# First group of an FNet and quick-GELU kernel: steps 2 to 7 built in one PSUM bank by a seed and two matrices, and the middle column's weights taken from summed rows

## Chip, cores and metric

One NeuronCore of a Trainium2 chip. The metric is the device time of one execution in microseconds (us). All arithmetic is in float32.

## What is computed

```python
X = np.fft.fft(x, axis=1)             # x: (8, 3008, 256), float32
X = np.fft.fft(X, axis=2)
x = X.real.astype(np.float32).reshape(8 * 3008, 256)
h = x @ w_in                          # w_in:  (256, 2048)
g = h * (1.0 / (1.0 + np.exp(-1.702 * h)))
out = (g @ w_out).astype(np.float32)  # w_out: (2048, 256)
```

The real part of a two-dimensional Fourier transform, then two matrix products with a sigmoid form of GELU between them. The kernel takes `w_in` and `w_out` as 64-bit numbers and makes float32 of them itself.

## The kernel before

The transform over the 3008 rows is done in two stages (47 x 64). The first folds rows and multiplies by a table on TensorE; its output is written to a DRAM scratch `Td` (`spill_first`) and read back in another order (`fill`, line 358, tile `t`, 512 KB a piece). `rotate` (psr) treats the middle column of it, and `stage2` (line 378, ps) makes the second stage; VectorE transposes the result into `pq` (line 385), which has two parts, the cosine part `pq[:, 0]` and the sine part `pq[:, 1]`. The transform over the 256 columns is folded into the weights: `fold_w(n)` multiplies a quarter of `w_in` (512 hidden units) by a cosine and sine table `cd` into psw and copies it to `wcs[0]` and `wcs[1]` on ScalarE (line 508). For quarters 1 to 3 it works on sums and differences of two row halves (`halved`, lines 480 and 481, on VectorE).

A step t is two blocks of 128 hidden units on 256 columns of output rows. Eight steps (NP = 8) are a group; 48 groups make the batch of 8 (three blocks `blk` and two halves `hh` each). Each hidden unit is needed for a row and for its mirrored row: with pa = `wcs[0]`ᵀ`pq[:, 0]` and pb = `wcs[1]`ᵀ`pq[:, 1]`, plus a term of one middle column (`nb`, a copy of row 0 of the sine part broadcast to all partitions, times a weight per hidden unit, `af1` and `af2 = 2 af1`), they are a sum and a difference. `first_row(n)` computes those weights per hidden unit for quarter n with 16 matmuls of one column (psf) and copies them on ScalarE (lines 516, 517).

The kernel has two ways to do it:

- In the first group (steps 0 to 7): `hidden(t)` puts pa and pb into two PSUM banks and copies pa to `v` on ScalarE (line 552); `rows(t)` adds v and pb on VectorE (582), forms `dif` from `nb`, `af2` and pb (587, twice) and adds it to pa (589); `activate(t)` applies GELU to both halves at once (593, 128x1024, in place). Row 0 of `wcs[1]` is not cleared until `no_row`, which has two DMAs.
- From step 8 on: `middle(t)` seeds one bank x with `nb` times `af1` on ScalarE (602, two instructions); `begin(t, 0)` and `begin(t, 1)` add both matrices into the same bank; between the two, `doubled(t)` copies twice the bank to `g` (614, ScalarE); `forward(t)` applies GELU to the bank (617), `backward(t)` subtracts it from g on VectorE (621), `activate_back(t)` applies GELU to that (624). Here row 0 of `wcs[1]` has to be zero.

`product(t, lo, hi)` multiplies the activated rows by `w_out` (o, line 191; all matmuls but those of line 378, 501, 701 go through the helper `halves`, line 191, each as two halves of 64 columns). From step 8 the products use a form with fewer matmuls, which needs differences of `w_out` (`differences`, line 493 on GpSimd; `small_weights`, line 712 on VectorE) and of the activations (632, 633, 639, 640).

Conversion of a chunk of weights (four of `w_in`, in0 to in3; four of `w_out`, out0 to out3) takes these operations of 128x1024: `sizes` (absolute value of the upper word, on ScalarE, line 429, or on VectorE, line 431), `clamp` (GpSimd, 435), `low` (lower word scaled, ScalarE, 439), `high` (two on VectorE, 454 and 455), and `finish`: `finish_in` (467) or `finish_out` (475, two), both on GpSimd. `bounds` is prepare, sizes on ScalarE, clamp, low.

Nothing is scheduled automatically: each engine executes its instructions in the order in which the program issues them, and that order is written by hand. Ahead of step 0 it is a straight list; for steps 0 to 7 it is `SCRIPT`, one list per step, after which the operations in `extra` for that step are issued (loads, `differences(i)` after steps 5 to 8, `small_weights(i)` after steps 7 to 10, `stage2` of the next block after step 8); from step 8 it is the loop's own order. A product is issued three steps (LAG = 3) after its hidden values. PSUM banks are handed out in turn from the list `spare`; `ring` does the same for SBUF buffers, of which the ring "h" (activated rows) shares its memory with `made`, the first stage's output that `spill_first` writes to DRAM. `warm(n)` issues n matmuls of 128x512 on one weight tile whose result nobody reads.

Of the kernel before, what the change touches and what calls it, by code (L numbers as in the profile page):

```python
# [27 lines left out]
F32 = mybir.dt.float32  # L28
# [91 lines left out]
def kernel(ctx: ExitStack, tc, x, w_in, w_out, tab1, tab2, out):  # L120
# [33 lines left out]
    af1, af2 = (const.tile([128, NF], F32, tag=f"af{i}", name=f"af{i}") for i in (1, 2))  # L154
    ones = const.tile([128, 128], F32, tag="ones", name="ones")
    twos = const.tile([128, 1], F32, tag="twos", name="twos")

    psu = ExitStack()
    o_banks = [psp.tile([128, 512], F32, tag=f"o{i}", name=f"o{i}") for i in range(2)]
# [16 lines left out]
    def bank(name, tag=None):  # L176
        if tag is None:
            tag = spare.pop(0)
            spare.append(tag)
        if tag in ("o0", "o1"):  # L180
            return o_banks[int(tag[1])]
        return (rest if tag[0] == "o" else psp).tile([128, 512], F32, tag=tag, name=name)
# [5 lines left out]
    def halves(out, lhs, rhs, **how):  # L188

        for c0 in (0, 64):  # L190
            nc.tensor.matmul(out[c0:c0 + 64], lhsT=lhs[:, c0:c0 + 64], rhs=rhs, skip_group_check=True, **how)  # L191
# [142 lines left out]
    def spill_first(k, m0, m1, engines):  # L334
        for c, eng in enumerate(engines):
            eng.dma_start(out=view(Td[0], (NJ * m0 + 16 * c + 12 - 4 * k) * D, [NJ * D, m1 - m0], [1, 4 * D]),
                          in_=made[k][64 * c + m0:64 * c + m1].rearrange("p q d -> p (q d)"))
# [3 lines left out]
            for p0, p1 in ROWS:  # L341
                nc.sync.dma_start(out=w1[64 * r + p0:64 * r + p1, :], in_=tab1[p0:p1, n0 + 4:])

    def warm(n):

        ps = bank("warm")
        for _ in range(n):
            nc.tensor.matmul(ps[:], lhsT=wcs[0][:, 0:128], rhs=wcs[0][:, 0:512], start=True, stop=True)

# [10 lines left out]
    def rotate(b, a0=0, a1=NG, copy=None):  # L360

        col = t4t[b][:, a0:a1, H]
        ps = bank("psr")
        halves(ps[:, 0:a1 - a0], rot, col, start=True, stop=True)
        (copy or nc.vector.tensor_copy)(col, ps[:, 0:a1 - a0])
# [111 lines left out]
    def halved(n):  # L477

        s = summed[n] = pre["in", n][0]
        nc.vector.tensor_tensor(s[:, 0:512], wst[n][:, 0], wst[n][:, 1], op=ALU.add)  # L480
        nc.vector.tensor_tensor(s[:, 512:], wst[n][:, 0], wst[n][:, 1], op=ALU.subtract)
# [29 lines left out]
    def first_row(n):  # L511

        ps = bank("psf")
        for f in range(4 * n, 4 * n + 4):
            halves(ps[:, f:f + 1], wcs[1][:, f * 128:f * 128 + 128], twos[:], start=True, stop=True)
        nc.scalar.copy(af2[:, 4 * n:4 * n + 4], ps[:, 4 * n:4 * n + 4])
        nc.scalar.activation(af1[:, 4 * n:4 * n + 4], ps[:, 4 * n:4 * n + 4], ACTF.Copy, scale=0.5)


    def no_row(c0):  # L520
        nc.sync.dma_start(out=wcs[1][0:1, c0:c0 + 1024], in_=tab1[127:128, n0 + 4:n0 + 1028])

    NP = NF // 2
    steps = [(b, blk, hh, p) for b in range(B) for blk in range(NBLK) for hh in range(2) for p in range(NP)]
# [19 lines left out]
    def hidden(t):  # L544

        n = width(t)
        pa, pb = (bank(name, f"b{i}" if t == NP - 3 else None) for i, name in enumerate(("pa", "pb")))
        for ps, cs in ((pa, 0), (pb, 1)):
            for i in range(2):
                halves(ps[:, i * 256:i * 256 + n], *operands(t, cs, i), start=(i == 0), stop=(i == 1))  # L550
        v = sp.tile([128, 512], F32, tag="v", name="v")
        nc.scalar.copy(two(v[:], n), two(pa[:], n))
        vb[t] = v, pa, pb
# [37 lines left out]
    def activate(t):  # L591
        g = free(ht[t][:], 0, [256, 4], [1, width(t)])
        nc.scalar.activation(g, g, ACTF.Gelu_apprx_sigmoid)

    def middle(t):

# [297 lines left out]
    for i, need in enumerate(((0, 7), (1,), (6,), (2,), (5,), (3,), (4,), ())):  # L894
        for g in need:
            fold_first(g)
        mix_first(i)
        if i == 0:
            warm(3)
            spare[:] = spare[5:] + spare[:5]  # L900
        if i % 2:
            spill_first(i // 2, 0, 16, (nc.sync, nc.scalar))
        if i == 3:
            sizes(in0, nc.scalar, 0, 512)
            clamp(in0, 0, 512)
        if i in (4, 7):
            low(in0, 512 * (i // 7), 512)
        if i == 6:
            sizes(in0, nc.vector, 512, 512)
            clamp(in0, 512, 512)  # L910
            for h0 in (0, 512):
                high(in0, h0, 512)
# [16 lines left out]
    load_out(1, nc.sync)  # L929
    fill(0, 4, NG)  # L930
    warm(1)
    fold_w(0)
    halved(1)
    rotate(0, 0, 4, nc.scalar.copy)
    prepare(out0)
    sizes(out0, nc.scalar)
# [19 lines left out]
    out1, in3, out2, out3 = ("out", 1), ("in", 3), ("out", 2), ("out", 3)  # L956
    for t, c in ((1, 2), (3, 3)):
        at(t, load_out, c, nc.sync)
    at(3, no_row, 0)
    at(3, load_matrices)  # L960
    if B > 1:
        for k in range(3):
# [9 lines left out]
    for b in range(B):  # L972
# [26 lines left out]
        for blk in range(NBLK):  # L999
            nxt = (b, blk + 1) if blk + 1 < NBLK else (b + 1, 0)  # L1000
            if nxt[0] < B:
                at(t0 + blk * NF + 8, stage2, *nxt)
                at(t0 + blk * NF + 9, nyquist_out, *nxt)
                at(t0 + blk * NF + 10, nyquist, *nxt)

    SCRIPT = (
        [(prepare, in2), (low, in2), (nyquist, 0, 0), (rows, 0, ((sizes, in2, nc.vector), (clamp, in2)))],
        [(first_row, 1), (activate, 0), (rows, 1), (high, in2), (finish, in2)],
        [(activate, 1), (rows, 2), (halved, 2)],
        [(product, 0, 0, None), (product, 1, 0, None), (bounds, out1), (activate, 2), (bounds, in3), (rows, 3), (activate, 3),  # L1010
         (fold_w, 2), (high, out1), (finish, out1), (high, in3), (finish, in3)],
        [(first_row, 2), (rotate, 0, 4, NG, nc.scalar.copy), (rows, 4), (halved, 3)],
        [(product, 2, 0, None), (activate, 4), (bounds, out2), (rows, 5), (activate, 5), (fold_w, 3), (high, out2), (finish, out2)],
        [(first_row, 3), (product, 3, 0, None), (bounds, out3), (rows, 6), (activate, 6), (high, out3), (finish, out3)],
        [(product, 4, 0, None), (rows, 7)])
    for t in range(n + LAG):
        if t < NP:
            if t == NP - 3:
                spare[:] = [tag for tag in spare if tag[0] == "o"] + ["b2"]
            if t == NP - 1:  # L1020
                middle(NP)
            hidden(t)
            if t == NP - 1:
                begin(NP)
                no_row(1024)
            for fn, *args in SCRIPT[t]:
                fn(*args)
            if t == NP - 1:
                doubled(NP)
                middle(NP + 1)  # L1030
        else:
            after, special = (any(fn in (mix1, stage2) for fn, _ in extra.get(k, ())) for k in (t - 1, t))
            if t < n:
                begin(t, 1)
            if t == NP:
                activate(t - 1)
            if after and t + 1 < n:
                middle(t + 1)
            if t < n:
                forward(t)  # L1040
            while waiting:
                m, ps = waiting.pop()
                mixed(m, 1, ps)
            opening = (t - LAG) % NP == 0 and t >= NP + LAG
            one, other = (t - LAG, (1, 2, 4, 7)), (t - LAG - 1, (5, 6, 3))
            if opening:
                small_products(*other)
            cut = 0 if opening and not after else 3 if after else 2
            product(t - LAG, 0, cut)
            if after:  # L1050
                small_products(one[0], one[1][:1])
                small_products(other[0], () if opening else other[1][:1])
            if t + 1 < n:
                begin(t + 1)
            if not opening:
                small_products(other[0], other[1][after:])
            product(t - LAG, cut, 6 if t - LAG == last else None)
            small_products(one[0], one[1][after:])
            swap(t - LAG - 2)
            if t < n:  # L1060
                backward(t)
            if t + 1 < n:
                doubled(t + 1)
            if t < n:
                activate_back(t)
                sums(t, nc.gpsimd)
            if t + 2 < n and not special:
                middle(t + 2)
            combine_small(t - LAG - 1)
            if t - LAG == last:  # L1070
                product(last, 6, None)
            sums(t - 1, nc.vector)
            deeper(t - 2, 0)
            deeper(t - 3, 1)
        if t == NP:
            psu.close()
            low = ctx.enter_context(tc.tile_pool(name="low", bufs=1, space=PS))
            pot["low"] = low.tile([128, 3 * 512], F32, tag="low", name="low")
        if t >= LAG:
            combine(t - LAG)  # L1080
            combine_last(t - LAG - 2)
            turn_last(t - LAG - 3, 0)
            turn_last(t - LAG - 4, 1)
        if t >= NP:
            spare[:] = [f"b{t % 2}"] * special + ["b2"]
        for fn, args in extra.get(t, ()):
            fn(*args)
# [28 lines left out]
```

## Time and profile before

| | us |
|---|---|
| median of 3 timed runs | 1846.71 |
| lowest and highest of them | 1846.24, 1849.34 |
| profiled execution, its time | 1845.24 |
| profiled execution, span from first to last instruction | 1843.5 |
| TensorE busy | 1826.2 |
| VectorE busy | 1479.1 |
| ScalarE busy | 1139.4 |
| GpSimd busy | 997.7 |

The mean granted TensorE clock of the profiled execution is 0.997 of full speed. PE is the TensorE matmul, PEld its weight load, DVE is VectorE, ACT ScalarE, POOL GpSimd, SP the sync engine that issues most DMAs. A row of a timeline gives the start, the length, engine and line, the operation, output and input tiles, shape and how many; a bracket gives the idle time of that engine just ahead and the instruction or DMA that ended it. Line numbers are those of the kernel before.

### The profile page before, as it was taken

The page shows a single profiled execution, that of the slowest core. Times are in us where ns is not written, and L with a number is a line of the kernel's source. Part 1 is how long each engine was busy: PE and PEld are TensorE (multiplying, and loading weights), DVE is VectorE, ACT ScalarE, POOL GpSimd, SP SyncE. Part 2 cuts the span into 40 slices and gives each one's busy share as a digit, 9 for nine tenths or more (in the row PEclk, how much of TensorE's full clock was granted, in tenths as well). Part 3 has the DMA queues.
Part 4 walks back from the last instruction along what each step waited for, and adds up shares of the span by engine and source line. Part 5 has one row for each costly group of instructions (what it writes and reads, how often), then busy time and mean ns, then how long its engine had stood idle before and what let it go on. Part 6 is the DMA issues. An engine that isn't in the chain of part 4 may idle for free.

```text
span 1843.5 us, 55849 instructions
## 1 busy us (share of the span) xinstructions
PE 1826.2 (99%) x23650; PEld 1398.9 (76%) x23650; DVE 1479.1 (80%) x1930; ACT 1139.4 (62%) x2231; POOL 997.7 (54%) x1068
## 2 busy tenths in 40 slices
PE   8999999999999999999999999999999999999998
PEld 4677777777777777777777777777777877778776
DVE  6888788887888778877888778878888788878874
ACT  4666656666666666666666666666656666556663
POOL 3785555554656546564456644666446654444442
PEclk9999999999999999999999999999999999999999
DMA  8721331114211151211502115020241102100101
GB/s 276 189 70 26 90 65 28 55 32 106 43 48 40 35 112 30 61 35 45 111 13 73 33 50 97 23 72 26 75 74 28 29 26 59 28 19 13 23 19 24
DMA packets 150841, 105.95 MB, mean 57 GB/s; under 512 B 106197, under 2 KB 131799, under 8 KB 150032
## 3 DMA queue, kind: packets, MB, share of 16 engines
q1 hardware_dynamic: 147760, 100.33, 22.6%
q8 instruction: 186, 3.05, 0.7%
q10 hardware_dynamic: 2832, 2.05, 0.5%
q14 instruction: 63, 0.52, 0.1%
HBM read 65.07 MB, written 48.05 MB: 61 GB/s over the span
## 4 chain that ended last, share of the span: by engine, by line
PE 95%; POOL 2%; DMA 1%; DVE 1%; issue 0%; ACT 0%; ACTq 0%; DVEq 0%; POOLq 0%; SPq 0%
PE x L191 35%; PE o L191 26%; PE low L701 25%; PE o L701 4%; PE ps L268 2%; PE ps L378 1%; DMA xt<-in_x_dram 1%; PE po L191 0%; DMA big<-in_moe_w_in_dram 0%; PE psw L501 0%; POOL wo L475 0%; PE pa L191 0%; POOL wo L493 0%; POOL big L632 0%; DMA t<-Td 0%
## 5 line engine op out<-in xcount | busy, mean ns | idle before, releaser
L632 POOL TENSOR_TENSOR big<-big 128x256 f32<-128x256 f32 (+1 forms) x376 | 353.6, 940 | 785.7 <-ACT big L624 672.2
L191 PE MATMUL x<-pq,wcs 128*64 128x256 f32 (+1 forms) x6016 | 768.8, 376 | 1.5 <-ACT g L614 0.9
L191 PE MATMUL o<-big,wo 128*64 128x256 f32 (+1 forms) x4800 | 621.0, 375 | 0.5 <-DVE big L639 0.5
L191 PEld LDWEIGHTS x<-pq,wcs 128*64 128x64 f32 x6016 | 414.1, 137 | 181.4 <-issue 15.6
L614 ACT ACTIVATE g<-x 128x512 f32<-128x512 f32 (+1 forms) x376 | 221.7, 590 | 380.1 <-PE x L191 378.9
L191 PEld LDWEIGHTS o<-big,wo 128*64 128x64 f32 x4800 | 341.8, 137 | 146.8 <-DVE big L639 0.9
L633 POOL TENSOR_TENSOR big<-big 128x256 f32<-128x256 f32 (+1 forms) x376 | 411.2, 1094 | 0.0
L621 DVE TENSOR_TENSOR big<-g,x 128x512 f32<-128x512 f32 (+1 forms) x376 | 250.7, 667 | 183.6 <-ACT big L617 183.4
L602 ACT ACTIVATE x<-nb,af 128x256 f32<-128x256 f32 (+1 forms) x752 | 353.0, 469 | 70.1 <-DVE pq L385 57.0
L701 PE MATMUL low<-big 128*64 128x128 f32 (+1 forms) x5888 | 381.4, 270 | 0.0
L701 PEld LDWEIGHTS low<-big 128*64 128x64 f32 x5888 | 336.9, 137 | 28.2
L617 ACT ACTIVATE big<-x 128x512 f32<-128x512 f32 (+1 forms) x376 | 219.2, 583 | 122.2 <-PE x L191 112.2
L663 DVE TENSOR_TENSOR big<-big 128x1024 f32<-128x1024 f32 (+1 forms) x184 | 235.4, 1280 | 65.9 <-PE low L701 43.1
L624 ACT ACTIVATE big<-big 128x512 f32<-128x512 f32 (+1 forms) x376 | 231.6, 616 | 34.9 <-DVE big L621 32.6
L701 PE MATMUL low<-big,wo 128*64 128x128 f32 (+1 forms) x2944 | 220.3, 270 | 0.1
L665 DVE TENSOR_TENSOR big<-big 128x512 f32<-128x512 f32 (+1 forms) x184 | 179.6, 976 | 16.3 <-DVE big L663 0.5
L667 DVE TENSOR_TENSOR big<-big 128x512 f32<-128x512 f32 (+1 forms) x184 | 184.0, 1000 | 0.0
L701 PEld LDWEIGHTS low<-big,wo 128*64 128x64 f32 x2944 | 171.8, 137 | 4.2 <-DVE big L667 0.5
L640 DVE TENSOR_TENSOR big<-big 128x512 f32<-128x512 f32 (+1 forms) x188 | 143.3, 762 | 6.5
L639 DVE TENSOR_TENSOR big<-big 128x512 f32<-128x512 f32 (+1 forms) x188 | 131.2, 698 | 3.5 <-POOL big L632 3.5
L803 DVE TENSOR_TENSOR big<-big,low 128x512 f32<-128x512 f32 (+3 forms) x184 | 109.0, 609 | 3.8
L701 PEld LDWEIGHTS o<-big,wo 128*64 128x64 f32 x1472 | 92.3, 137 | 24.9
(104 smaller groups left out, 1100.5 us busy)
## 6 DMA issues: line engine op xcount, KB each, us to landing
out_dram<-os SPq DMA_DIRECT2D x284, 64.0 KB
t<-Td SPq DMA_DIRECT2D x22, 512.0 KB
Td<-xt SPq DMA_DIRECT2D x56, 192.0 KB
xt<-in_x_dram SPq DMA_DIRECT2D x14, 512.0 KB
xt<-Xr SPq DMA_DIRECT2D x14, 512.0 KB
nb<-Nd SPq DMA_DIRECT2D x23, 256.0 KB
out_dram<-os SPq DMA_DIRECT2D x96, 56.0 KB
Xr<-in_x_dram SPq DMA_DIRECT2D x7, 752.0 KB
```

The costliest lines, as they stand in the source:

```text
L191: nc.tensor.matmul(out[c0:c0 + 64], lhsT=lhs[:, c0:c0 + 64], rhs=rhs, skip_group_check=True, **how)
L602: nc.scalar.activation(x[:, i * 256:i * 256 + n], nbt[b, blk][:, hh * 256:hh * 256 + n], ACTF.Copy, scale=af1[:, f:f + 1])
L614: nc.scalar.activation(two(g[:], n), two(xb[t][:], n), ACTF.Copy, scale=2.0)
L617: nc.scalar.activation(front(t), two(xb[t][:], width(t)), ACTF.Gelu_apprx_sigmoid)
L621: nc.vector.tensor_tensor(back(t), two(gt.pop(t)[:], n), two(xb.pop(t)[:], n), op=ALU.subtract)
L624: nc.scalar.activation(back(t), back(t), ACTF.Gelu_apprx_sigmoid)
L632: eng.tensor_tensor(right(t, S1, n), left(t, A21, n), right(t, A22, n), op=ALU.add)
L633: eng.tensor_tensor(left(t, S3, n), left(t, A11, n), left(t, A21, n), op=ALU.subtract)
L663: nc.vector.tensor_tensor(free(big[:], SUM, *both_), free(big[:], from11 + w, *twice), free(big[:], from11, [at_right(t, 0) + w - from11, ...
L665: nc.vector.tensor_tensor(s2, a11, s1, op=ALU.subtract)
L667: nc.vector.tensor_tensor(s4, a12, s2, op=ALU.subtract)
L701: nc.tensor.matmul(o, lhsT=lhs, rhs=rhs, start=first_in, stop=(p == NP - 2), skip_group_check=True)
```

## The change

- Steps 2 to 7 of the first group use `middle`, `begin`, `doubled` and a function `plain` (forward, backward, and GELU on the backward half) as later steps do, one bank a step; steps 0 and 1 keep `hidden`, `rows` and `activate`.
- `SCRIPT` is written anew for that: products 1 to 4 are cut in two or three parts and put between the parts of the steps; which banks are free is set by hand (`banks`); `hidden` and the seeds of step 8 and 9 move into it.
- `first_row(n)` for quarters 1 to 3 takes its weights from the summed rows of `halved(n)` times `signs` (twice a column of `cd`), ahead of `fold_w(n)`; that column of `cd` is then zeroed, so `fold_w` leaves row 0 of `wcs[1]` zero for these quarters and `no_row` clears only the first 512 columns.
- Three filler matmuls (`warm(3, "o2")`) stand between `halved(1)` and `rotate`, on a bank of their own.
- The sizes of out1, in3, out2 and out3 are taken on VectorE (`ready`) and no longer on ScalarE (`bounds`), with `low` issued later by itself; `low(in2)` stands behind `activate(0)`.
- One of the two DMAs of the last `spill_first` of this kind (i = 7) goes from the sync engine's queue to ScalarE's.

```diff
--- before.py
+++ after.py
@@ -154,6 +154,7 @@
+    signs = const.tile([128, 1], F32, tag="signs", name="signs")
 
     psu = ExitStack()
     o_banks = [psp.tile([128, 512], F32, tag=f"o{i}", name=f"o{i}") for i in range(2)]
@@ -341,9 +342,9 @@
             for p0, p1 in ROWS:
                 nc.sync.dma_start(out=w1[64 * r + p0:64 * r + p1, :], in_=tab1[p0:p1, n0 + 4:])
 
-    def warm(n):
-
-        ps = bank("warm")
+    def warm(n, tag=None):
+
+        ps = bank("warm", tag)
         for _ in range(n):
             nc.tensor.matmul(ps[:], lhsT=wcs[0][:, 0:128], rhs=wcs[0][:, 0:512], start=True, stop=True)
 
@@ -512,13 +513,16 @@
 
         ps = bank("psf")
         for f in range(4 * n, 4 * n + 4):
-            halves(ps[:, f:f + 1], wcs[1][:, f * 128:f * 128 + 128], twos[:], start=True, stop=True)
+            if n in summed:
+                halves(ps[:, f:f + 1], free(summed[n], f - 4 * n, [4, 128]), signs[:], start=True, stop=True)
+            else:
+                halves(ps[:, f:f + 1], wcs[1][:, f * 128:f * 128 + 128], twos[:], start=True, stop=True)
         nc.scalar.copy(af2[:, 4 * n:4 * n + 4], ps[:, 4 * n:4 * n + 4])
         nc.scalar.activation(af1[:, 4 * n:4 * n + 4], ps[:, 4 * n:4 * n + 4], ACTF.Copy, scale=0.5)
 
 
-    def no_row(c0):
-        nc.sync.dma_start(out=wcs[1][0:1, c0:c0 + 1024], in_=tab1[127:128, n0 + 4:n0 + 1028])
+    def no_row():
+        nc.sync.dma_start(out=wcs[1][0:1, 0:512], in_=tab1[127:128, n0 + 4:n0 + 516])
 
     NP = NF // 2
     steps = [(b, blk, hh, p) for b in range(B) for blk in range(NBLK) for hh in range(2) for p in range(NP)]
@@ -544,7 +548,7 @@
     def hidden(t):
 
         n = width(t)
-        pa, pb = (bank(name, f"b{i}" if t == NP - 3 else None) for i, name in enumerate(("pa", "pb")))
+        pa, pb = bank("pa"), bank("pb")
         for ps, cs in ((pa, 0), (pb, 1)):
             for i in range(2):
                 halves(ps[:, i * 256:i * 256 + n], *operands(t, cs, i), start=(i == 0), stop=(i == 1))
@@ -591,6 +595,24 @@
     def activate(t):
         g = free(ht[t][:], 0, [256, 4], [1, width(t)])
         nc.scalar.activation(g, g, ACTF.Gelu_apprx_sigmoid)
+
+    def plain(t, what):
+
+        n = width(t)
+        if what == "forward":
+            h = ht[t] = ring("h").rearrange("p (a f n) -> p a f n", a=2, f=2)
+            nc.scalar.activation(two(h[:], n), two(xb[t][:], n), ACTF.Gelu_apprx_sigmoid)
+            return
+        other = two(ht[t][:, 1, 0], n)
+        if what == "backward":
+            nc.vector.tensor_tensor(other, two(gt.pop(t)[:], n), two(xb.pop(t)[:], n), op=ALU.subtract)
+        else:
+            nc.scalar.activation(other, other, ACTF.Gelu_apprx_sigmoid)
+
+    def ready(key):
+        prepare(key)
+        sizes(key, nc.vector)
+        clamp(key)
 
     def middle(t):
 
@@ -899,7 +921,7 @@
             warm(3)
             spare[:] = spare[5:] + spare[:5]
         if i % 2:
-            spill_first(i // 2, 0, 16, (nc.sync, nc.scalar))
+            spill_first(i // 2, 0, 16, (nc.scalar if i == 7 else nc.sync, nc.scalar))
         if i == 3:
             sizes(in0, nc.scalar, 0, 512)
             clamp(in0, 0, 512)
@@ -929,8 +951,11 @@
     load_out(1, nc.sync)
     fill(0, 4, NG)
     warm(1)
+    nc.scalar.activation(signs[:], cd[:, 0, 1, 0:1], ACTF.Copy, scale=2.0)
     fold_w(0)
+    nc.vector.memset(cd[:, 0, 1, 0:1], 0.0)
     halved(1)
+    warm(3, "o2")
     rotate(0, 0, 4, nc.scalar.copy)
     prepare(out0)
     sizes(out0, nc.scalar)
@@ -956,7 +981,7 @@
     out1, in3, out2, out3 = ("out", 1), ("in", 3), ("out", 2), ("out", 3)
     for t, c in ((1, 2), (3, 3)):
         at(t, load_out, c, nc.sync)
-    at(3, no_row, 0)
+    at(3, no_row)
     at(3, load_matrices)
     if B > 1:
         for k in range(3):
@@ -1003,37 +1028,35 @@
                 at(t0 + blk * NF + 9, nyquist_out, *nxt)
                 at(t0 + blk * NF + 10, nyquist, *nxt)
 
+    def banks(*tags):
+        spare[:] = tags
+
+    fwd, bwd, act = ((lambda t, what=what: plain(t, what)) for what in ("forward", "backward", "again"))
+    copy_row = rotate, 0, 4, NG, nc.scalar.copy
     SCRIPT = (
-        [(prepare, in2), (low, in2), (nyquist, 0, 0), (rows, 0, ((sizes, in2, nc.vector), (clamp, in2)))],
-        [(first_row, 1), (activate, 0), (rows, 1), (high, in2), (finish, in2)],
-        [(activate, 1), (rows, 2), (halved, 2)],
-        [(product, 0, 0, None), (product, 1, 0, None), (bounds, out1), (activate, 2), (bounds, in3), (rows, 3), (activate, 3),
-         (fold_w, 2), (high, out1), (finish, out1), (high, in3), (finish, in3)],
-        [(first_row, 2), (rotate, 0, 4, NG, nc.scalar.copy), (rows, 4), (halved, 3)],
-        [(product, 2, 0, None), (activate, 4), (bounds, out2), (rows, 5), (activate, 5), (fold_w, 3), (high, out2), (finish, out2)],
-        [(first_row, 3), (product, 3, 0, None), (bounds, out3), (rows, 6), (activate, 6), (high, out3), (finish, out3)],
-        [(product, 4, 0, None), (rows, 7)])
+        [(banks, "b1", "b2", "o2", "o3", "o4", "o2"), (hidden, 0), (prepare, in2), (nyquist, 0, 0), (rows, 0, ((sizes, in2, nc.vector), (clamp, in2)))],
+        [(hidden, 1), (activate, 0), (low, in2), (rows, 1), (first_row, 1), (ready, out1), (activate, 1), (middle, 2), (high, in2),
+         (finish, in2)],
+        [(product, 0, 0, None), (begin, 2), (doubled, 2), (high, out1), (product, 1, 0, 4), (middle, 3), (low, out1), (finish, out1),
+         (begin, 2, 1), (fwd, 2), (begin, 3), (bwd, 2), (doubled, 3), (act, 2), (halved, 2)],
+        [(product, 1, 4, None), (ready, in3), (begin, 3, 1), (fwd, 3), (banks, "o4", "o2", "o3", "b2"), (first_row, 2), (bwd, 3), (act, 3),
+         (middle, 4), (fold_w, 2), (low, in3), (high, in3), (finish, in3)],
+        [(product, 2, 0, 4), (begin, 4), (doubled, 4), (product, 2, 4, None), (middle, 5), (ready, out2), (begin, 4, 1), (fwd, 4), (begin, 5),
+         (bwd, 4), (doubled, 5), (act, 4), (low, out2), (halved, 3), copy_row],
+        [(product, 3, 0, 4), (begin, 5, 1), (fwd, 5), (banks, "o4", "o2", "o3", "b2"), (first_row, 3), (bwd, 5), (act, 5), (middle, 6),
+         (fold_w, 3), (product, 3, 4, None), (high, out2), (finish, out2)],
+        [(begin, 6), (doubled, 6), (product, 4, 0, 3), (middle, 7), (ready, out3), (begin, 6, 1), (fwd, 6), (begin, 7), (bwd, 6), (doubled, 7),
+         (act, 6), (low, out3), (high, out3), (finish, out3), (banks, "b2")],
+        [(middle, NP), (product, 4, 3, 6), (begin, 7, 1), (fwd, 7), (begin, NP), (bwd, 7), (doubled, NP), (act, 7), (middle, NP + 1),
+         (product, 4, 6, None)])
     for t in range(n + LAG):
         if t < NP:
-            if t == NP - 3:
-                spare[:] = [tag for tag in spare if tag[0] == "o"] + ["b2"]
-            if t == NP - 1:
-                middle(NP)
-            hidden(t)
-            if t == NP - 1:
-                begin(NP)
-                no_row(1024)
             for fn, *args in SCRIPT[t]:
                 fn(*args)
-            if t == NP - 1:
-                doubled(NP)
-                middle(NP + 1)
         else:
...
```

More of the change, by code (lines that the diff above doesn't have):

```diff
@@ L1034 @@
                 begin(t, 1)
-            if t == NP:
-                activate(t - 1)
             if after and t + 1 < n:
```

## Prediction

> **What bounds the kernel now.** I read the page first: busy time by engine, the busy slices, the chain that ended last.
>
> ```profile
> PE 1826.2 (99%) x23650; PEld 1398.9 (76%) x23650; DVE 1479.1 (80%) x1930; ACT 1139.4 (62%) x2231; POOL 997.7 (54%) x1068
> ...
> PE   8999999999999999999999999999999999999998
> ...
> PE 95%; POOL 2%; DMA 1%; DVE 1%; issue 0%; ACT 0%; ACTq 0%; DVEq 0%; POOLq 0%; SPq 0%
> ```
>
> TensorE carries 95% of the chain, and only the first and last slices show holes. The edit leaves the 23650 matmuls as they are but for three fillers, so it can act only through TensorE's holes in the first 100 us: what TensorE is late by near 100 us, the end is late by. So next, TensorE's timeline from 24 to 64 us (start, length, in brackets the idle time ahead and who ended it).
>
> ```profile
> 31.72 0.29 PE L191 MATMUL psr<-t,small 128*64 128x4 f32 x4 [2.64 <-DMA t<-Td]
> 31.94 1.96 PE L378 MATMUL ps<-t,small 64*32 64x128 f32 x64
> 33.83 1.02 PE L191 MATMUL psf<-twos,wcs 128*64 128x1 f32 x16
> 34.70 3.66 PE L501 MATMUL psw<-big,small 128*64 128x512 f32 x8
> ...
> 43.58 1.08 PE L191 MATMUL pa<-pq,wcs 128*64 128x256 f32 x8 [0.27 <-DVE big L589]
> ...
> 47.06 7.11 PE L191 MATMUL o<-big,wo 128*64 128x256 f32 x64
> ...
> 61.15 1.08 PE L191 MATMUL pb<-pq,wcs 128*64 128x256 f32 x8 [1.92 <-DVE big L589]
> ```
>
> Three waits of 2.64, 0.27 and 1.92 us. The same shapes are shorter later (ps 1.19, psf 0.58, psw 1.92), and the busy time by stretch says why (PE, PEld, DVE, ACT, POOL, then granted clock and DMA share).
>
> ```profile
> 28.45:31.87 3.42, 0.78 (x8) 0.18 (x4) 3.35 (x4) 0.99 (x2) 1.78 (x2) 1.00 0.90 290
> 31.87:38.70 6.83, 6.83 (x96) 3.77 (x96) 4.63 (x9) 3.36 (x7) 2.48 (x3) 0.50 0.96 369
> ...
> 59.17:62.59 3.42, 1.50 (x16) 1.22 (x16) 2.02 (x5) 2.14 (x3) 3.16 (x2) 1.00 1.04 294
> 44.50:84.10 39.60, 37.68 (x358) 25.68 (x354) 32.79 (x49) 25.97 (x39) 25.89 (x23) 1.00 0.86 224
> ```
>
> After 3.42 us with 0.78 of matmul the clock is 0.50 for 6.83 us; after 3.42 us with 1.50 it stays at 1.00. Last, the chain of waits from 66 us, which is not TensorE's: it is the weight preparation.
>
> ```profile
> 66.40 1.24 DVE big L455
> 67.78 2.50 POOL wo L475 x2
> ...
> 73.17 1.02 POOL big L435
> 74.94 1.24 DVE big L455
> 76.31 2.52 POOL wo L475 x2
> ...
> 84.97 0.95 DVE big L712
> 87.58 0.98 PE x L191 x8
> ```
>
> So, whatever TensorE gains before 60 us, step 8's products at 87.58 start only when the last two output chunks are split, finished and differenced.
>
> **The fillers.** warm(3) costs some 2.84 us (the row of the earlier three at 11.65); they can start once the first folded weights are copied, near 29.4, and end at 32.0, in the wait of 2.64. psr slips by 0.2 to 0.3. The clock then should not fall: rows ps, psf, psw and pa (1.30 against 1.08) lose 0.77 + 0.44 + 1.74 + 0.22 = 3.2 us. Against that, psw would now wait for the summed weights (DVE L480 and L481 at 33.31 and 33.92, released by POOL, unmoved): 0.9. TensorE ends hidden(0), psn, hidden(1) and psf(1) near 43.3 - 3.2 + 0.9 + 0.2 = 41.2 instead of 43.3.
>
> **What is late next.** Next in the new order is product(0), which needs activate(0). Three timelines (DVE, POOL, ACT) say when that can be.
>
> ```profile
> 40.42 0.69 DVE L582 TENSOR_TENSOR big<-v,pb 128x512 f32<-128x512 f32 x1 [2.06 <-PE pb L191]
> 41.03 0.68 DVE L431 TENSOR_SCALAR big<-big 128x1024 uint32<-128x1024 uint32 x1
> ```
>
> ```profile
> 38.53 2.52 POOL L475 TENSOR_TENSOR wo<-big 128x512 uint32<-128x512 uint32 x2 [2.16 <-PE psw L501]
> ```
>
> ```profile
> 43.48 1.06 ACT L593 ACTIVATE big<-big 128x1024 f32<-128x1024 f32 x1
> ```
>
> L582 loses its wait on pb, but its buffer is read by a spill that lands near 39.4, so it gains 1.0 at most. Behind it L431 (sizes of in2) meets POOL's L475, which ends at 41.05. DVE operations on SBUF alone stretch beside POOL (L480 took 1.52 beside a POOL clamp, 0.69 alone; L455 2.18 against 1.23), so I leave L431's end at 41.7, then L587, L589, and gelu(0) at 43.5 to 44.5. Before, TensorE filled that time with hidden(2), hidden(3); the new list puts product(0) first. So TensorE idles about 3.4 us (41.1 to 44.5), and at 44.5 it is behind, not ahead: before, 0.95 us of hidden(2) was done by then. **+0.95.**
>
> **Steps 2 to 7.** Matmuls are equal: 16 of 128x256 a step, two matrices into one bank. ACT loses the copy (0.58) and the wide gelu (1.06), and gets two seeds of 0.469, the doubled copy 0.590, forward 0.583, backward's gelu 0.616: 1.64 becomes 2.73. DVE loses 0.69 + 0.87 + 0.69 and gets one subtraction of 0.67. The sizes of four chunks go from ACT (1.18) to DVE (0.68). Over the stretch 44.5 to 84.1 that is ACT +6.5 - 4.7 = +1.8 on 25.97 busy of 39.60, DVE -9.5 + 2.7 = -6.8 on 32.79: neither becomes the bound, so the order decides. Laying the new order engine by engine with these durations, the 1.92 and some 0.36 in small pieces go; new are 0.37 (psw(2) on DVE's sums), 0.20, 0.43 and 0.35 (product(4) on POOL's finish of out2) and 1.15 (step 8 on ACT, whose gelus queue ahead of its seed): 2.5. Net +0.2; at ps (84.10 before) TensorE is **+1.1** behind.
>
> **The weights chain.** Before, high(out2) starts on DVE at 65.68, behind step 5's rows. Now it stands behind backward(5), which needs forward(5), which needs begin(5,1). Up to that TensorE has, from 44.5: 112 output matmuls and 64 hidden ones at 0.108 (19.0), psw 1.7, psf and psr 0.6, waits 0.6, so 66.4; forward until 67.2, backward until 67.9, so high(out2) at 67.9: +2.2. From there the rows of the chain above follow each other, each 2.1 to 2.4 later (POOL's first L475 at 69.9, its second at 78.5), and the products of 87.58 come **+2.3**. The later of 1.1 and 2.3 counts, and from about 90 us TensorE has no hole to give it back in.
>
> **The rest.** psf still has 16 small matmuls; signs (0.17, as L517) lies in ACT's wait of 2.33 ahead of L365; the memset (0.27, as L1087) in DVE's wait of 1.38 ahead of L480; without that cover, up to 0.3. no_row's second copy leaves SP's queue. The spill half moved from SP to ACT costs ACT an issue of 0.36 where ACT has 2.4 of 3.42 free; its landing could move the t<-Td wait by -0.5 to +0.5; I take 0, as 0.96 of the DMA time is in use either way.
>
> **The clock again.** The idle of 3.4 us is longer than the 2.64 that halved the clock. How much of a 3.42-us window it empties depends on where windows begin. A window that is over 0.23 busy has a chance to keep the clock, one of 0.44 keeps it; with the limit midway it falls for some 60% of the offsets. Then 6.83 us of dense work go at half speed: at most 3.4, less the 0.6 of waits that shrink, less up to 1.2 where part of the low stretch lies in the idle time: 1.7 to 2.9, I take 2.3. The chain moves with it, since it now hangs on begin(5,1).
>
> The Trainium skill ("TensorE: Matmul & The Clock Gate", Part 1 on the clock gate) says that the clock falls after at least one whole idle window of about 3.4 us, free-running. By that rule, 3.4 us of idle would almost never empty a window and the change would cost 2.3 alone. The row at 28.45 disagrees, having 0.78 of matmul in the window, so I follow the row.
>
> **Sum.** 2.3 + 2.3 = +4.6 on the profiled execution: 1845.24 becomes 1849.8. The median of the timed runs, 1846.71, lies 1.5 above that execution: 1851.3. Under 0.2% (3.7 us) a measurement of this kernel can't tell a change from none.
>
> **Rivals.**
> - The clock holds: +2.3, 1849.0, within 0.2%. For it: the window's offset is chance. Against: 3.4 us is longer than 2.64. 0.33.
> - Faster: gelu(0) comes when TensorE does. That needs L431 before POOL's second L475 and the spill landed by 38.5; it decides if gelu(0) starts before 41.5. Then 2.64 + 3.2 + 1.92 + 0.27 go and 2.5 come, if high(out2) follows up: -5.5, 1841.2. Against: three unmoved rows hold gelu(0). If only TensorE follows and the chain keeps 2.2 of its delay, -1, 1845.7. 0.13 and 0.05.
> - Slower still: ACT in order becomes the pace of steps 2 to 7, each adding its 1.1 to the path: 6.6, 1853.3. Against: ACT has 13.6 us free in the stretch. 0.07.
>
> That the filler and the new order would not take effect is no rival: the instruction lists show them as written.
>
> **Numbers.** Likeliest: 1851.3, chance 0.42. Slower 0.42 + 0.07 = 0.49; same 0.33 + 0.05 = 0.38; faster 0.13. The range takes all but the lower part of the fast case and the tail over the slow one: 1842.9 to 1853.5; the likeliest case alone 1850 to 1852.5.
>
> **What would show it.** In the profile after: no low clock from 31.87, ps 1.2 and psf 0.58 there; psr near 32.2; an idle of 3 to 4 us ahead of the first o, released by ACT's gelu at about 44.5, then 6.83 us at 0.50 (or none, in the rival); L454 of out2 near 68 to 70. I am wrong if the first o starts before 42, or if high(out2) is not later than 66.

## The result and the profile after

The changed kernel takes 1849.24 us (median of 14 runs, 1847.13 to 1852.94), the kernel before 1846.07 (14 runs of the same job): a ratio of 1.0017, 95% interval 1.0009 to 1.0025, so slower by some 3 us. The predicted sign is right and the time is inside the range; 1851.3 was 2 us too much. The median lies below the 1850 to 1852.5 of the likeliest case, close to the 1849.0 of the rival in which the clock holds, and the loss of 0.17% is under the 0.2% that the prediction set as its limit; the interval of 14 runs still keeps it apart from no change.

The profiled execution has a span of 1846.8 us and a time of 1848.78, against 1843.5 and 1845.24. The page of the changed kernel, busy time and chain (its line numbers are higher by one to 22: L191 is now L192, 454 455, 455 456, 475 476, 582 586, 593 597, 602 624):

```profile
PE 1829.1 (99%) x23656; PEld 1408.7 (76%) x23656; DVE 1474.6 (80%) x1917; ACT 1140.5 (62%) x2246; POOL 1000.5 (54%) x1068
...
PE 95%; DMA 2%; POOL 2%; DVE 1%; issue 0%; ACT 0%; SPq 0%; DVEq 0%; POOLq 0%; ACTq 0%
```

Nothing in the averages tells where the time goes: TensorE is busy 2.9 us more, and the fillers alone are 2.84; ACT and DVE moved by 1 and 5 us, and neither is the bound. TensorE's timeline does:

```profile
29.80 2.84 PE L349 MATMUL warm<-wcs 128*128 128x512 f32 x6
33.25 0.28 PE L192 MATMUL psr<-t,small 128*64 128x4 f32 x4 [0.60 <-DMA t<-Td]
33.46 1.19 PE L379 MATMUL ps<-t,small 64*32 64x128 f32 x64
34.58 0.63 PE L192 MATMUL psf<-twos,wcs 128*64 128x1 f32 x16
...
44.76 5.36 PE L192 MATMUL o<-big,wo 128*64 128x256 f32 x32 [1.95 <-ACT big L597]
...
56.83 1.04 PE L192 MATMUL psf<-signs,big 128*64 128x1 f32 x16
...
80.23 0.98 PE L192 MATMUL x<-pq,wcs 128*64 128x226 f32 x8 [1.04 <-ACT x L624]
...
91.89 0.98 PE L192 MATMUL x<-pq,wcs 128*64 128x226 f32 x8 [1.44 <-ACT x L624]
```

The fillers lie in the old wait of 2.64 us, and ps and psf behind it have their full-clock lengths. The first o waits for ScalarE's GELU until 44.76, as forecast for 44.5. But it then takes 5.36 us for 32 matmuls, where 64 took 7.11 before; psf from the summed rows takes 1.04 and not 0.58; and the x that was at 87.58 is at 91.89, behind a wait of 1.44. By stretch (PE, PEld, DVE, ACT, POOL, clock, DMA):

```profile
41.75:45.16 3.41, 1.46 (x19) 1.33 (x18) 3.34 (x8) 1.60 (x2) 2.42 (x2) 1.00 0.92 339
45.16:48.57 3.41, 3.41 (x20) 2.40 (x17) 2.98 (x4) 2.43 (x6) 1.34 (x1) 0.50 1.07 382
```

The clock falls to 0.50, but for 3.41 us and not for 6.83. The chain of waits around the weight preparation (L455 and L456 are `high`, L476 is `finish_out`, L734 `small_weights`, and the last row leads to the x at 91.89):

```profile
69.06 0.69 DVE big L608
69.74 0.62 DVE big L455
70.38 1.25 DVE big L456
71.77 2.82 POOL wo L476 x2
...
79.24 1.24 DVE big L456
80.62 2.71 POOL wo L476 x2
...
89.29 0.95 DVE big L734
90.24 0.64 DVE pq L386
```

backward(5) (L608) stands right ahead of high(out2) (L455, L456), and each later link is 4.0 to 4.3 us behind its row of before (67.78, 76.31, 87.58). From there the distance stays: the same ScalarE instruction (forward, L617 and L639) is 4.31 us later at step 9, 4.34 at 700 us, 4.05 at 840 us and 3.55 at the end.

### The profile page after: what moved, and what is told of

It reads as the page before. It is cut to its first block, busy times and chain, and to the rows that moved or that the text cites. A ratio compares the mean times of both kernels' runs of the same rounds, so it can differ in the third digit from the quotient of the medians.

```text
span 1846.8 us, 55855 instructions
## 1 busy us (share of the span) xinstructions
PE 1829.1 (99%) x23656; PEld 1408.7 (76%) x23656; DVE 1474.6 (80%) x1917; ACT 1140.5 (62%) x2246; POOL 1000.5 (54%) x1068
## 4 chain that ended last, share of the span: by engine, by line
PE 95%; DMA 2%; POOL 2%; DVE 1%; issue 0%; ACT 0%; SPq 0%; DVEq 0%; POOLq 0%; ACTq 0%
PE x L192 35%; PE o L192 27%; PE low L723 25%; PE o L723 4%; PE ps L269 2%; PE ps L379 1%; DMA xt<-in_x_dram 1%; DMA Td<-big 1%; PE po L192 0%; POOL wo L476 0%; DMA big<-in_moe_w_in_dram 0%; POOL wo L494 0%; POOL big L654 0%; PE psw L192 0%; DVE big L456 0%
## 5 line engine op out<-in xcount | busy, mean ns | idle before, releaser
L192 PE MATMUL x<-pq,wcs 128*64 128x256 f32 (+1 forms) x6112 | 781.6, 376 | 3.7 <-ACT x L624 2.9
L192 PE MATMUL o<-big,wo 128*64 128x256 f32 (+1 forms) x4800 | 624.9, 376 | 2.6 <-ACT big L597 2.0
L192 PEld LDWEIGHTS x<-pq,wcs 128*64 128x64 f32 x6112 | 424.6, 137 | 183.8 <-issue 15.6
L636 ACT ACTIVATE g<-x 128x512 f32<-128x512 f32 (+1 forms) x382 | 225.5, 590 | 386.8 <-PE x L192 385.3
L192 PEld LDWEIGHTS o<-big,wo 128*64 128x64 f32 x4800 | 345.2, 137 | 148.4 <-POOL big L436 2.0
L624 ACT ACTIVATE x<-nb,af 128x256 f32<-128x256 f32 (+1 forms) x764 | 358.7, 470 | 71.2 <-DVE pq L386 57.9
L639 ACT ACTIVATE big<-x 128x512 f32<-128x512 f32 (+1 forms) x376 | 219.3, 583 | 119.4 <-PE x L192 108.8
```

What stands on the lines that cost most here:

```text
L624: nc.scalar.activation(x[:, i * 256:i * 256 + n], nbt[b, blk][:, hh * 256:hh * 256 + n], ACTF.Copy, scale=af1[:, f:f + 1])
L636: nc.scalar.activation(two(g[:], n), two(xb[t][:], n), ACTF.Copy, scale=2.0)
L639: nc.scalar.activation(front(t), two(xb[t][:], width(t)), ACTF.Gelu_apprx_sigmoid)
```

## Experiments

All are timed in five rounds beside the kernel before; ratios are to that. Medians of the kernel before were 1846.67, 1846.42 and 1846.54 in the three jobs.

### Fillers ahead of product(0)

```diff
-(first_row, 1), (ready, out1), (activate, 1)
+(first_row, 1), (warm, 2, "o0"), (ready, out1), (activate, 1)
```

> The changed kernel with two more filler matmuls on a free bank between psf(1) and product(0), in TensorE's idle time ahead of the first o (1.95 us in the trace). First theory (the end hangs on TensorE from 44.8 us on, through begin(5,1) and the chain of weight preparation behind it): no granted clock of 0.50 after 45 us, the first 32 o matmuls take 3.5 us and not 5.36, begin(5,1) and everything behind it comes 1.7 us earlier, and the time is 1.5 to 1.7 us below the changed kernel's 1849.2. Rival (the clock loss is covered by waits that come later, as most of the 3.2 us were before): the o matmuls are quicker, but the step that starts at 91.89 stays where it is, time as the changed kernel's.

Measured: 1848.96, ratio 1.0012 (1.0003 to 1.0020), so about 0.9 us below the changed kernel by the ratios and 0.3 by the medians, inside both intervals and less than the 1.5 to 1.7 expected. The trace is clearer: no low clock after the start, and the 32 o matmuls take 3.67 us.

```profile
44.08 3.67 PE L192 MATMUL o<-big,wo 128*64 128x256 f32 x32
```

The x is at 90.35, 1.54 earlier. Of the 0.68 earlier start and the 1.7 of clock some 0.85 are lost again: psf of quarter 2 is 2.22 us earlier than in the changed kernel (54.61 against 56.83), psr behind it 1.65 (63.83 against 65.48). That fits the small waits of 0.37 and 0.20 that the prediction laid out there, which the low clock covers. So in these two traces the low clock is on the path with some 0.9 of its 1.7 us (1.54 - 0.68), if the earlier start kept its whole worth; the times are too coarse to confirm it.

### high(out2) ahead of backward(5)

```diff
-[(product, 3, 0, 4), (begin, 5, 1), ... (product, 3, 4, None), (high, out2), (finish, out2)]
+[(high, out2), (finish, out2), (product, 3, 0, 4), (begin, 5, 1), ... (product, 3, 4, None)]
```

> The changed kernel with high(out2) and finish(out2) issued at the head of step 5, ahead of backward(5) instead of behind it. First theory (the weights chain is late because high(out2) stands behind backward(5) in VectorE's order): finish_out(2) starts near 69.4 and not 71.77, the wait of 1.44 us ahead of the x at 91.89 shrinks to 0.2, time 1.2 us below the changed kernel's (about 1848.0). Rival (TensorE's own pace to 91 us sets the end, and the chain only follows it): finish_out(2) earlier, but another wait of the same length ahead of that x, time unchanged.

Measured: 1847.11, ratio 1.0006 (0.9997 to 1.0015). VectorE's timeline shows the new place, TensorE's the wait that is left:

```profile
66.96 0.69 DVE L455 TENSOR_SCALAR big<-big 128x1024 uint32<-128x1024 uint32 x1
67.68 1.23 DVE L456 SCALAR_TENSOR_TENSOR big<-big 128x1024 uint32<-128x1024 uint32 x1
68.82 0.68 DVE L608 TENSOR_TENSOR big<-g,x 128x512 f32<-128x512 f32 x1
```

```profile
90.01 0.98 PE L192 MATMUL x<-pq,wcs 128*64 128x226 f32 x8 [0.34 <-ACT x L624]
```

finish_out(2) starts at 69.06 (expected 69.4) and the wait goes from 1.44 to 0.34 (expected 0.2). No other wait takes its place, so the rival falls. The median is 2.1 lower, more than the 1.2 expected. The trace's own execution has its low clock at 27.34 us and none behind 45, which for the rest leaves the clock as one explanation; five rounds don't separate the two.

### psf from dense rows

```diff
-halves(ps[:, f:f + 1], free(summed[n], f - 4 * n, [4, 128]), signs[:], start=True, stop=True)
+halves(ps[:, f:f + 1], summed[n][:, (f - 4 * n) * 128:(f - 4 * n) * 128 + 128], signs[:], start=True, stop=True)
```

> The changed kernel with the stationary operand of psf for quarters 1 to 3 read in dense rows of the sums instead of every fourth element; the hidden units are thereby in the wrong order for the middle column's weights, all else is as before. First theory (psf takes 1.04 instead of 0.58 us because its weight load of every fourth element takes 217 ns and not 138): psf rows back at 0.6 us, TensorE 0.9 us earlier at begin(5,1), time 0.9 to 1.4 us below the changed kernel's. Rival (the load is slow for another reason, such as DMA traffic or VectorE at the same buffer): psf stays at 1.04 us and the time too.

Measured: 1848.77, ratio 1.0009 (1.0000 to 1.0019), on the time alone undecided. The instruction rows of tile psf, in the changed kernel and then in this one's timeline:

```profile
L192 PEld LDWEIGHTS psf<-signs,big x48: 192/217/218, 41.0 to 68.9; 128*64 128x64 f32 x48
...
L192 PEld LDWEIGHTS psf<-twos,wcs x16: 132/138/138, 34.6 to 35.0; 128*64 128x64 f32 x16
```

```profile
57.38 0.61 PE L192 MATMUL psf<-signs,big 128*64 128x1 f32 x16
...
92.23 0.98 PE L192 MATMUL x<-pq,wcs 128*64 128x226 f32 x8 [1.44 <-ACT x L624]
```

The stride of four is the cause of the longer psf (217 against 138 ns a load). The forecast gain of 0.9 or more is not in the trace, and the times (0.5 below the changed kernel by the medians, 1.5 by the ratios) don't decide it: product(0) starts 0.55 later here (45.31), and the x is 0.34 later, so 0.2 is won. psf(1) lies ahead of the wait for GELU and psf(3) behind begin(5,1); only psf(2) is on the path. It gives 0.43 (begin(5,1) at 67.45, 67.33 in the changed kernel), and 0.2 of that is lost again behind it, in L456 (1.31 us, 1.24 there) and L476 (2.97, 2.82 there).

### The kernel before with the fillers, and with fillers and psf

```diff
...
     halved(1)
+    warm(3, "o2")
     rotate(0, 0, 4, nc.scalar.copy)
```

> The kernel before with the three filler matmuls alone, ahead of rotate, on bank o2. First theory (most of the low clock's 3.2 us from 31.87 is covered, as the weights chain sets the x at 87.58): no 0.50 clock from 31.87, ps 1.2 and psf 0.58 us there, the x at 87.58 at most 0.4 us earlier, time 0.0 to 0.5 us below that of before. Rival (TensorE's loss there is on the path): everything 2.5 to 3.2 us earlier, about 1843.2.

Measured: 1847.10, ratio 1.0001 (0.9992 to 1.0010). No low clock, ps 1.20 and psf 0.63, and then a new wait, which is the rival's refutation:

```profile
43.91 1.08 PE L191 MATMUL pa<-pq,wcs 128*64 128x256 f32 x8 [1.98 <-DVE big L589]
```

The wait of 0.27 ahead of hidden(2) has become 1.98: VectorE's rows don't come earlier. The 3.2 us of clock were covered.

```diff
+    nc.scalar.activation(signs[:], cd[:, 0, 1, 0:1], ACTF.Copy, scale=2.0)
     fold_w(0)
     halved(1)
+    warm(3, "o2")
...
-            halves(ps[:, f:f + 1], wcs[1][:, f * 128:f * 128 + 128], twos[:], start=True, stop=True)
+            if n in summed:
+                halves(ps[:, f:f + 1], free(summed[n], f - 4 * n, [4, 128]), signs[:], start=True, stop=True)
+            else:
+                halves(ps[:, f:f + 1], wcs[1][:, f * 128:f * 128 + 128], twos[:], start=True, stop=True)
```

> The kernel before with the three filler matmuls and psf of quarters 1 to 3 taken from the summed rows (the sine column stays in place, so all steps of the first group keep hidden, rows and activate). It is the change without the one-bank steps and the new order. First theory (the slower psf costs only what lies ahead of the weights chain; the rest of the change's loss is the new order): psf rows of 1.04 us for quarters 1 to 3, time 0.0 to 0.9 us above the kernel before. Rival (the psf rows are the loss): 1.4 us or more above it.

Measured: 1845.86, ratio 0.9999 (0.9990 to 1.0008), with psf rows of 1.00 and 1.01 us. Fillers and summed rows together cost nothing that shows in this order of work. By that the loss lies in what this kernel leaves out: the one-bank steps with their order, the sizes on VectorE, and the spill on one queue.

### The changed kernel without its fillers, and with the spill on two queues

```diff
     halved(1)
-    warm(3, "o2")
     rotate(0, 0, 4, nc.scalar.copy)
```

> The changed kernel without the three fillers ahead of rotate. First theory (product(0) waits for gelu(0) near 44.5 us whatever TensorE does before, so the low clock between 32 and 39 us is covered, and the fillers only move the low clock to the stretch behind 45 us, where it costs): wait of 2.6 us ahead of psr, clock 0.50 from about 32 us, less than 1.3 us of idle ahead of product(0), no low clock after it, time 0 to 1.5 us below the changed kernel's 1849.2. Rival (the low clock at 32 us costs its 3.2 us): 1851 to 1852.4.

Measured: 1847.72, ratio 1.0008 (0.9999 to 1.0017). The rival's 1851 is out. Wait of 2.45 ahead of psr, low clock from 35.05 to 38.47, idle ahead of product(0) 1.05, no low clock behind it. The x is at 91.80 (91.89 in the changed kernel): without the fillers the kernel is no slower. Its median is 1.5 lower, but the intervals of the two ratios overlap.

```diff
-spill_first(i // 2, 0, 16, (nc.scalar if i == 7 else nc.sync, nc.scalar))
+spill_first(i // 2, 0, 16, (nc.sync, nc.scalar))
```

> The changed kernel with the last spill of the first stage on the sync engine's and ScalarE's queues again, as in the kernel before. First theory (it lands somewhat earlier, which only lengthens the wait for gelu(0)): from the end of the last copy of e to the landing of its spill about 3.2 us and not 4.0, psr up to 0.9 us earlier, time within 0.5 us of the changed kernel's 1849.2. Rival (the late landing shifts all that follows): 0.7 to 0.9 us below it.

Measured: 1848.33, ratio 1.0014 (1.0006 to 1.0023). From the end of the copy of e to the issue of the load that waits for its spill it is 3.2 us (24.86 to 28.04), and 4.3 with both halves on ScalarE's queue (24.81 to 29.08). The first o starts at 43.88, 0.88 earlier than in the changed kernel, after copies of e that end within 0.05 us of each other, as the rival had it. One pair of traces says too much, though: over all of them that stretch is 3.2 to 3.9 us in the five with the spill on two queues and 3.4 to 5.3 in the eight with it on one. What it does to the time (0.5 by the ratios, 0.9 by the medians) lies between the two expectations and stays open.

### Both output chunks ahead of the step work

```diff
-[(product, 3, 0, 4), (begin, 5, 1), ... (product, 3, 4, None), (high, out2), (finish, out2)],
-[(begin, 6), ... (ready, out3), (begin, 6, 1), ... (act, 6), (low, out3), (high, out3), (finish, out3), (banks, "b2")],
+[(high, out2), (finish, out2), (ready, out3), (product, 3, 0, 4), (begin, 5, 1), ... (product, 3, 4, None), (low, out3)],
+[(high, out3), (finish, out3), (begin, 6), ... (begin, 6, 1), ... (act, 6), (banks, "b2")],
```

> The changed kernel with the last two output chunks ahead of the step work: high(out2), finish(out2), sizes(out3) and clamp(out3) at the head of step 5, low(out3) at its end, high(out3) and finish(out3) at the head of step 6. First theory (the end hangs on the weights chain; with it out of the way, on TensorE's pace): finish_out(3) starts before 76 and not at 80.62, no wait ahead of the x of step 10 (1.44 in the changed kernel) and less than 0.3 ahead of step 8's (1.04), time 2.2 to 2.9 us below the changed kernel's 1849.2, that is about 1846.6, and 0.3 to 0.9 below that with high(out2) alone moved. Rival (only high(out2)'s place counted): the same time as with high(out2) alone moved, 1847.1.

Measured: 1845.79, ratio 0.9997 (0.9988 to 1.0006), 3.7 below the changed kernel by the ratios, more than expected: it is level with the kernel before. No wait is left ahead of step 8's or step 10's x. finish_out(3), expected before 76, starts at 79.87 in the trace; that execution has the clock at 0.50 for 6.83 us from 45.20, and is the slowest of the eleven (1848.54). The last kernel below, which has the same order without that, has 76.99, so the forecast of 76 was about 1 us too early.

### Step 2 ahead of product(0), alone and with the rest

```diff
-(hidden, 0), (prepare, in2), (nyquist, 0, 0), (rows, 0, ((sizes, in2, nc.vector), (clamp, in2)))
-(hidden, 1), (activate, 0), (low, in2), (rows, 1), (first_row, 1), (ready, out1), (activate, 1), (middle, 2), ...
-(product, 0, 0, None), (begin, 2), (doubled, 2), ...
+(first_row, 1), (hidden, 0), (prepare, in2), (nyquist, 0, 0), (rows, 0), (sizes, in2, nc.vector), (clamp, in2)
+(hidden, 1), (middle, 2), (begin, 2), (activate, 0), (low, in2), (rows, 1), (ready, out1), (activate, 1), ...
+(product, 0, 0, None), (doubled, 2), ...
```

> The changed kernel with TensorE's idle ahead of product(0) filled with work of step 2: psf(1) ahead of hidden(0), middle(2) and begin(2) ahead of activate(0) and product(0), and sizes(in2) on VectorE behind rows(0) and not within it. First theory (gelu(0) holds product(0), and begin(5,1) and the weights chain hang on TensorE from there): product(0) starts by 44.2, 8 matmuls of x done before it, begin(5,1) and all behind it 1.0 to 1.7 us earlier where the clock is the same, time about 1847.8. Rival (the idle costs nothing, since what follows waits for the loaded and converted chunks anyway): the waits of 1.04 and 1.44 us grow by what was won, time 1849.

Measured: 1847.69, ratio 1.0008 (0.9999 to 1.0017); 1847.8 was expected. The 8 x matmuls come before product(0), though behind a wait of 0.71, and product(0) starts at 46.14 and not by 44.2, in an execution that is late from its loads on (POOL's first finish of in1 at 31.79, 31.13 in the changed kernel). The waits of 1.01 and 1.44 ahead of the x of steps 8 and 10 are as they were, so they did not swallow the gain. In the trace a new wait did, and psf of quarter 2 starts where it did in the changed kernel (56.83):

```profile
56.82 1.13 PE L192 MATMUL psf<-signs,big 128*64 128x1 f32 x16 [0.97 <-DVE big L481]
```

On top of that and of both output chunks ahead:

```diff
-spill_first(i // 2, 0, 16, (nc.scalar if i == 7 else nc.sync, nc.scalar))
+spill_first(i // 2, 0, 16, (nc.sync, nc.scalar))
```

> Both of the two last edits in one kernel (output chunks ahead of the step work; begin(2), psf(1) and sizes(in2) moved around product(0)), and the last spill on two queues as in the kernel before. First theory: the gains add up, 2.2 to 2.9 and 1.0 to 1.7, so 1844.6 to 1846.0, 0 to 2 us below the kernel before. Rival (TensorE has no more than its own waits to give, and these are gone with one of the edits): no lower than 1846.6.

Measured: 1846.16, ratio 0.9998 (0.9989 to 1.0006). The gains do not add: psf of quarter 2 waits 0.95 for VectorE's sums (L481), as in the kernel with step 2 ahead alone. The time lies between the two expectations, and with early_out at 1845.79 the combination has no gain that shows.

### Both output chunks ahead, and the gap filled

On top of the kernel with both output chunks ahead:

```diff
-(first_row, 1), (ready, out1), (activate, 1)
+(first_row, 1), (warm, 2, "o0"), (ready, out1), (activate, 1)
```

> The kernel with the last two output chunks ahead of the step work, and two fillers more on a free bank ahead of product(0). First theory (what it has left to lose is the low clock behind 45 us, in some executions): no granted clock of 0.50 after 45 us in the trace, no wait over 0.6 us on TensorE between 50 and 100 us, time 0.2 to 1.2 us below 1845.8, under the kernel before by 0.03 to 0.1%. Rival (the low clock is covered, or the fillers delay product(0) where TensorE is late): 1845.8 or above.

Measured: 1844.90, ratio 0.9991 (0.9982 to 1.0000): 1.6 us below the kernel before by medians and ratios, as expected. It is the only one whose interval does not reach above 1.0000, and it ends just there. TensorE by stretch:

```profile
45.60:49.00 3.40, 3.37 (x32) 2.75 (x34) 3.33 (x5) 2.85 (x6) 1.34 (x1) 1.00 1.08 381
50.00:100.00 50.00, 50.00 (x526) 35.53 (x524) 38.36 (x48) 31.96 (x64) 37.30 (x37) 1.00 0.74 165
```

From 50 to 100 us TensorE has no hole at all at full clock, where before had 1.92 us of waiting at 61.15. What it still loses there lies ahead of its first o, which starts at 45.63 behind a wait of 0.75 for GELU.

## Why the prediction was right, and where it was off

- **The fillers** do what was said: they fill the 2.64 us, and the 3.2 us of clock come back and are worth nothing by themselves (before_filler, no_filler).
- **What is late next**: right. gelu(0) starts at 43.56 (43.48 before), held by the spill that L586 waits for (it starts at 40.45), by L432 that stretches to 0.96 beside POOL, and by L591 and L593. The idle ahead of product(0) was to be 3.4 us; it is 1.95 in this execution and 1.05 to 3.00 in others with the same order. TensorE reaches the end of its work later than forecast, for three reasons: the execution is 0.64 late before the spill of e (copies of e at 23.74, 23.10 before); the spill takes 0.9 more until the load behind it is issued (4.27 us against 3.33), where the prediction took 0 with 0.5 either way; and psf(1) takes 1.0.
- **The clock again**: it fell as forecast, but in part by luck, and the term was mis-sized. The idle time was 1.95 us and not 3.4, and of the 3.41 us ahead of the fall 1.46 were busy, a share of 0.43, where the forecast let the clock hold from midway between 0.23 and 0.44. Of the 1.46, 1.0 is psf(1), one-column matmuls; the last section shows why that may not have counted. The forecast took 6.83 us at half speed from the kernel before, with 2.3 on the path; here it is one stretch of 3.41, worth 1.7 on TensorE (5.36 against 3.67 for 32 o), some 0.9 of it on the path by the estimate above. In some executions it is longer (6.83 in early_out's trace), in others absent. Among the 14 timed runs the three with a mean clock of 0.996 took 1851.95 to 1852.94, the two with 1.000 took 1847.64 and 1848.20. The fastest, 1847.13, has 0.998, and a mean does not say where the clock was low, so that the likeliest case and the rival in which the clock holds are mixed in the median is likely but not shown.
- **Steps 2 to 7**: "matmuls are equal" held for the steps, not for psf, where "still 16 small matmuls" was costed by their count; each costs 0.079 us more in its weight load. It was 0.4 us on the path. Of the small waits only 1.04 shows in the trace (1.15 was forecast); two others show in psf_dense (0.46 and 0.15 for POOL's finish of out2, forecast at 0.43 and 0.35), and VectorE's sums in no_filler and two_queues (0.24 and 0.19, forecast at 0.37).
- **The weights chain**: right, and the core of the loss. high(out2) at 69.66 was forecast as 67.9 plus what the clock adds; L476 at 71.77 and 80.62 against 69.9 and 78.5 plus the same. At 87.58 the sum of 4.6 stands against 4.31 measured. Moving the two chunks forward takes all of the loss back (early_out); moving high(out2) alone takes 2.0 of the 3.1 by the ratios (out2_first), part of which may be the clock.
- **The sum**: 4.6 was forecast and 4.31 is there at step 10, though with less from the clock and more from psf and the later start. That the two errors nearly cancel is luck. Of the 4.31, 3.3 is left at the end of the two profiled executions; where TensorE gives the 1.0 back, most of it behind 800 us, was not followed. And the step from the profiled execution to the median, 1.5, rested on three runs; with 14 runs the median of before is 1846.07, 0.8 above that execution. By the times the 4.6 became 3.54 (1848.78 - 1845.24) and the 1.5 became 0.46 (1849.24 - 1848.78): about 1 us each of the 2 by which 1851.3 was too high.

The Trainium skill ("TensorE: Matmul & The Clock Gate", Part 1 on the clock gate) has the clock fall after a whole idle window of about 3.4 us. No fall ahead of the kernel's end agrees: the stretch of 3.41 us ahead of each has 0.77 (before) to 1.99 us of matmul in it (no_filler, 31.64 to 35.05). One ahead of a fall, from the kernel before with fillers and psf, and one from the changed kernel, behind which the clock held:

```profile
57.48:60.89 3.41, 1.82 (x25) 1.21 (x25) 2.98 (x5) 1.25 (x5) 3.41 (x2) 1.00 1.04 367
```

```profile
89.53:92.94 3.41, 1.97 (x22) 1.11 (x20) 2.54 (x5) 1.37 (x3) 3.33 (x6) 1.00 0.00 1
```

By the rule the clock would have held; it fell in the changed kernel's trace with 1.46 of 3.41 us busy.

## To carry to other kernels

When steps are reordered, look at what is queued behind the new waits on each in-order engine: here two conversions of weights, which had nothing to do with the edit, stood behind a subtraction that now waits for TensorE and ScalarE. Filling an idle gap pays only if the next dependency moves too; otherwise the gap moves to that one, here from under a cover to a place without one. A stationary operand with a stride costs in its load, even where the matmul is of one column. And a stretch of one-column matmuls looks busy in a profile but, by the fit below, did not keep the clock up.

## What the runs showed of the hardware

- The clock fell after 3.41-us stretches with 0.77 to 1.99 us of matmul (eight traces) and stayed after others with 1.50 (before, 59.17 to 62.59) to 1.98 (two_queues, 42.22 to 45.63). So no limit on the busy time fits, neither the prediction's between 0.23 and 0.44 of a stretch nor a higher one. It stayed low for 3.41 us in six traces and for 6.83 in two (before and early_out).
- The work done fits where the busy time does not. Count each matmul by weight rows times weight columns times streamed columns, and let one of 128*64 weights and 256 columns count 0.108 us, its time in the dense stretches (6.91 us for the 64 o at 47.06 before). Step through each of the 13 traces in stretches of 3.4133 us, counted back from its last change of clock. Behind every stretch with up to 1.26 us of work the clock was 0.50, and behind every one with 1.29 or more it was 1.00, in all 6980 that the traces hold. The changed kernel's stretch from 41.75, with 1.46 us busy, has 0.34 us of work; the one from 59.17 before, with 1.50 busy, has 1.35. This gives the length too: the first low stretches of before and early_out had 1.10 and 1.26, and the clock stayed low; the others had 1.44 or more. The count was made after the runs, and none of them tested it.
- A weight load of 64 columns takes 138 ns from dense rows and 217 ns from every fourth float32.
- VectorE's L456 (128x1024) took 3.26 us in the changed kernel at 49.94, beside POOL's L468 from 49.47 to 52.11, and 1.23 at 59.82, alone.
